# Four seven-product units per tile from tile 3, in a written-out order, with the second product begun on plain h and two subtractions on GpSimd

## The chip, the cores and the metric

One core of one Trainium2 chip. The time is the device time of one execution in microseconds, from runs of the same program; beside it there is one execution recorded by the hardware profiler. Engines are called PE (TensorE; PEld is its weight load), DVE (VectorE), ACT (ScalarE), POOL (GpSimd) and SP (SyncE, which here only issues output transfers).

## What is computed

Attention over pooled keys and values, and behind it a two-layer network with SiLU (8 batches, 8 heads, 576 positions, head size 64; pool 8, so 72 pooled rows; 4608 tokens, width 512, hidden width 2048):

```python
k_p = k.reshape(B, H, Sp, pool, D).mean(axis=3)
v_p = v.reshape(B, H, Sp, pool, D).mean(axis=3)
scores = np.matmul(q, k_p.transpose(0, 1, 3, 2)) / sqrt(D)
attn = softmax(scores)
x = matmul(attn, v_p)              # to [4608, 512], heads side by side
h = x @ w_in                       # [4608, 2048]
g = h * (1.0 / (1.0 + np.exp(-h)))
out = g @ w_out                    # [4608, 512], float32
```

All weights, x and g are held in bfloat16; sums are float32.

## The kernel before, in words

The tokens are cut in nine tiles of 512, `t` = 0 to 8. In each tile the *first product* (`up`) makes h_T = silu(x w_in), transposed, and the *second product* (`down`, `down_quarters`) makes the output rows. While tile t is worked on, the attention of batch a = t + 1 is fed in between, so that the columns of xT are there for tile t + 1. Tiles 7 and 8 have no attention in them, as there is no batch 8.

**Seven products for eight.** From tile 1 on, both products use a scheme in which a 2 x 2 block product takes seven block products in place of eight, at the price of sums of blocks before it and of results after it. The products are numbered 1 to 7. They accumulate in three PSUM tiles: P takes products 2, 4 and 7, Q takes 5, 3 and 6, R takes 1. Between them P and Q are copied out, so that one bank serves two purposes.

- In the *first product* such a scheme is a **unit**: four groups of 128 hidden columns by 512 tokens by the whole width of 512. `UNITS` names three of them: groups 4 to 7, 8 to 11 and 12 to 15. Each product of a unit is four matmuls of 256 columns (L477). ScalarE copies P after product 2 to r_sb (L494); VectorE forms rr_sb = Q + r_sb after product 5 (L497), t_sb = R - rr_sb after product 1 (L500), c_sb[0] = P + t_sb after product 7 (L509) and c_sb[1] = Q + t_sb after product 6 (L512); ScalarE makes four Silu (L485), two of PSUM after products 4 and 3, two of c_sb ("h" and "s" in the order's letters). The sums of weight blocks (`unit_weight_sum`, L437) are made once, in tiles 0 and 1; the sums of x blocks (`unit_x_sum`, L444) once per tile, five of them, at the end of the tile before.
- Groups 0 to 3 are made by `plain` (L537): four groups of four matmuls of 512 columns each, and one Silu each (L543).
- In the *second product* each of the seven products is 16 matmuls of 256 columns (L645). The left sides are sums of blocks of h_T (`hidden_sum`, L605: for products 2, 5, 1, 6 and 7), or h_T itself (products 4 and 3). The weight sums are in w_sum. The order is 2, 5, 1, 4, 3, 7, 6; r_sb, rr_sb and t_sb are used here too (L658, L660, L664), and the output rows are collected in o_sb (L666, L671, L675, L679) and stored by `store` (L549).

**Order.** The program is scheduled by hand: each engine runs its instructions in the order in which they are emitted. For tiles 2 to 8 the order of the first product's stages is a string (`THREE`: letter A, B, C for the unit and the numbers for the stages, "g0" for a plain group). All other work is a *filler*, emitted when a step counter (one step per matmul group) reaches its number: hidden sums, transposes of q (`q_transpose`, L159), scores and their exponentials (`scores`, L340, L348), denominators (`denominators`, L358, L367, L368), numerators with the multiplications that write xT (`numerators`, L384, L393), x sums, and the table loads of ScalarE (`attn_tables`, `moe_tables`).

**GpSimd.** From tile 2 on GpSimd pools k and v of batch a (`pool_k`, `pool_v`; L190, L193). It does so behind `behind_x_sums` (L196), a copy of one element that makes it wait for the last x sum. GpSimd also issues the loads: q of batch a + 1 (`load_q`, L151 and, for the last batch, eight small ones at L144), the first half of the raw k and v rows (`load_one`, L180), and the second half, added on by the transfer to the first, so it waits until that has landed (`load_rest`, L184).

**PSUM.** The 8 banks are two groups: "at" with five (scores, denominators, numerators, the units' P and Q) and "mm" with three (the units' R, plain groups, the second product's P, Q and R). A new tile takes the next bank of its group in turn and waits for the readers of what was there.

**SBUF buffers shared by both products:** r_sb, rr_sb, t_sb and c_sb exist once.

The visits of attention in a tile are three thirds of the positions; the third numerators of a batch are made one tile later than its others (`numerators(a - 1, visits[2])`).

Of the kernel before, what the change touches and what calls it, by code (L numbers as in the profile page):

```python
# [27 lines left out]
FP32 = mybir.dt.float32  # L28
# [8 lines left out]
def kernel(  # L37
# [9 lines left out]
    nc = tc.nc  # L47
# [43 lines left out]
    def ps_tile(shape, dtype, tag, name):  # L91
        return psum.tile(shape, dtype, tag=tag, bufs=banks[tag], name=name)
# [24 lines left out]
            singles.tile([128, 5, 2, 256], BF16, name=f"w_sum1{n}") for n in range(2)  # L117
        )
    ]
    x_sum = singles.tile([128, 5, 2, NQ], BF16, name="x_sum")  # L120
    gate = singles.tile([128, 1], BF16, name="gate")
    c_sb = [singles.tile([128, 2, NQ], FP32, name=f"c_sb{n}") for n in range(2)]
# [54 lines left out]
    def load_one(b, name):  # L177
        st = batches.setdefault(b, {})
        raw = raw_tile(f"{name}_raw", H)
        nc.gpsimd.dma_start(out=raw, in_=source(b, name)[:, :, :PH])  # L180
        st[f"{name}_raw"] = raw
# [10 lines left out]
        )  # L192
        nc.gpsimd.tensor_add(out=dst, in0=raw[:, :, :D], in1=raw[:, :, D : 2 * D])  # L193

    def behind_x_sums():
        nc.gpsimd.tensor_copy(out=gate[:1], in_=x_sum[:1, U_XI[6], 0, :1])  # L196

    def pool_k(b):
        pool_rows(kp[:SP], batches[b]["k_raw"])
# [119 lines left out]
    def third(n):  # L319
        return tuple((g, n * QV, (n + 1) * QV) for g in range(2))  # L320
# [78 lines left out]
    def attn_tables():  # L399
        nc.scalar.preload_act_table_set("natural_log_exp_and_others")  # L400
# [13 lines left out]

    UNITS = ((4, 6), (8, 10), (12, 14))
    UW = [
        {
            (i, j): w_in_sb[:, 2 * j : 2 * j + 2, 128 * u : 128 * (u + 2)]  # L420
# [14 lines left out]
    def unit_weight_sum(y, n):  # L435
        a, b = U_W[n]
        nc.vector.tensor_tensor(  # L437
            out=w_sum1[y][U_WI[n]], in0=UW[y][a], in1=UW[y][b],
            op=ALU.subtract if n in (6, 7) else ALU.add,
        )  # L440
# [19 lines left out]
    def up(t, fillers, items):  # L460
        step = spread(
            fillers,
            sum(
                KF if len(it) == 3 else 2 * len(it[1].strip("hs")) for it in items
            ),
        )
        ps = {}

        def product(y, n, bank, first):
            if first:  # L470
                tag = "mm" if bank == "R" else "at"
                ps[y, bank] = ps_tile([128, 2, NQ], FP32, tag, f"u_ps{bank}")
            w, x = unit_weights(y, n), unit_x(t, n)
            for u in range(2):
                next(step)
                for kk in range(2):
                    nc.tensor.matmul(  # L477
                        ps[y, bank][:, u, :], lhsT=w[:, kk, 128 * u : 128 * (u + 1)],
                        rhs=x[:, kk, :], start=first and u == 0 and kk == 0,
                        stop=kk == 1, skip_group_check=True,  # L480
                    )

        def hidden(y, i, j, src):
            g = UNITS[y][i]
            nc.scalar.activation(  # L485
                h_T[:, g : g + 2, j * NQ : (j + 1) * NQ], src, func=AF.Silu
            )

        tt = nc.vector.tensor_tensor

        def stage(y, n):
            if n == "2":
                product(y, 2, "P", True)
                nc.scalar.copy(r_sb, ps[y, "P"])  # L494
            elif n == "5":
                product(y, 5, "Q", True)
                tt(out=rr_sb, in0=ps[y, "Q"], in1=r_sb, op=ALU.add)  # L497
            elif n == "1":
                product(y, 1, "R", True)
                tt(out=t_sb, in0=ps[y, "R"], in1=rr_sb, op=ALU.subtract)  # L500
            elif n == "4":
                product(y, 4, "P", False)
                hidden(y, 1, 0, ps[y, "P"])
            elif n == "3":
                product(y, 3, "Q", False)
                hidden(y, 0, 1, ps[y, "Q"])
            elif n == "7":
                product(y, 7, "P", False)
                tt(out=c_sb[0], in0=ps[y, "P"], in1=t_sb, op=ALU.add)  # L509
            elif n == "6":  # L510
                product(y, 6, "Q", False)
                tt(out=c_sb[1], in0=ps[y, "Q"], in1=t_sb, op=ALU.add)  # L512
            elif n == "h":
                hidden(y, 0, 0, c_sb[0])
            else:
                hidden(y, 1, 1, c_sb[1])

        for it in items:
            if len(it) == 3:
                plain(t, step, *it)  # L520
            else:
                for n in it[1]:
                    stage(it[0], n)
        for _ in step:
            pass

    def plain(t, step, g, n0, n):
        tag = "at" if (t, g, n0) == (0, 3, 0) else "mm"
        hp_ps = ps_tile([128, 512], FP32, tag, "hp_ps")
        c0 = (t * NTT + n0) % NX  # L530

        for r0, r1 in ((0, min(n, NX - c0)), (min(n, NX - c0), n)):
            for kk in range(KF) if r1 > r0 else ():
                if r0 == 0:
                    next(step)
                x0 = (c0 + r0) % NX
                nc.tensor.matmul(  # L537
                    hp_ps[:, r0:r1],
                    lhsT=w_in_sb[:, kk, g * 128 : (g + 1) * 128],
                    rhs=xT[:, kk, x0 : x0 + r1 - r0],  # L540
                    start=(kk == 0), stop=(kk == KF - 1),
                )
        nc.scalar.activation(h_T[:, g, n0 : n0 + n], hp_ps[:, :n], func=AF.Silu)  # L543
# [58 lines left out]
    def hidden_sum(n, k0, k1):  # L602
        a, b, op = H_SUMS[n]
        ks = slice(k0, k1)
        nc.vector.tensor_tensor(  # L605
            out=h_sum[n][:, ks, :], in0=quarter(*a, ks), in1=quarter(*b, ks), op=op
        )
# [17 lines left out]
    def left(n, kt, c):  # L625
        cs = slice(128 * c, 128 * (c + 1))
        if n in h_sum:
            return h_sum[n][:, kt, cs]
        i = n - 3
        return h_T[:, i * KQ + kt, i * NQ + 128 * c : i * NQ + 128 * (c + 1)]  # L630
# [55 lines left out]
            pass  # L686


    warm_ps = ps_tile([128, 512], FP32, "mm", "warm_ps")

    def warm_up(n):
# [97 lines left out]
        " C6 Ch Cs g2 g3",  # L789
    )  # L790
    visits = [third(n) for n in range(3)]
    for t in range(NT):
        a = t + 1
        f_up, f_down = [], []
        if t == 0:
            GA = 11
            items = [(g, 0, HS) for g in range(GA)]
            items += [(g, HS, NTT - HS) for g in range(GA)]
            items += [(g, 0, NTT) for g in range(GA, KG)]
            f_up += [(1, lambda: denominators(0, part(0, 1), on_dve=True))]  # L800
            f_up += [(5, lambda: denominators(0, part(1, 1), on_dve=True))]
            f_up += [(13, lambda: numerators(0, part(0, 1)))]
            f_up += [(17, lambda: numerators(0, part(1, 1)))]
        else:
            G = lambda *gs: [(g, 0, NTT) for g in gs]
            if t == 1:
                items = (
                    G(12, 13, 14, 15) + [(0, "25143"), (1, "2"), (0, "7"), (1, "5")]
                    + [(0, "6h"), (1, "1")] + G(0) + [(1, "4"), (0, "s"), (1, "3")] + G(1)
                    + [(1, "7h6")] + G(2) + [(1, "s")] + G(3)  # L810
                )
            else:
                items = []
                for it in THREE[t // B].split():
                    items += [(("BCA".index(it[0])), it[1])] if it[0] in "ABC" else G(int(it[1]))
            if t == 1:
                for n in U_X:
                    f_up.append((0, lambda n=n: unit_x_sum(t, n)))
            for n in (2, 5):
                h_at = 50 if t == B else 54 if t > 1 else 45  # L820
                f_up.append((h_at, lambda n=n: hidden_sum(n, 4, 8)))
            f_up.append((56, lambda: hidden_sum(6, 4, 8)))
            for n, k0 in ((2, 0), (5, 0), (1, 4), (1, 0)):
                f_up.append((64, lambda n=n, k0=k0: hidden_sum(n, k0, k0 + 4)))
            f_down.append((33, lambda: hidden_sum(7, 0, 8)))
            f_down.append((71 if t < B else 50, lambda: hidden_sum(6, 0, 4)))

        for n, t0, f_to, at, parts in (
# [71 lines left out]
        if t == 1:  # L900
            def unit_weight_tiles():
                k_w = big.tile([128, 4, 2, 256], BF16, tag="k_raw2", name="w_sum12")
                v_w = big.tile([128, 4, 2, 256], BF16, tag="v_raw2", name="w_sum12")
                w_sum1.append([k_w[:, i] for i in range(4)] + [v_w[:, 0]])

            f_down.append((72, unit_weight_tiles))
            for i, n in enumerate(U_W):
                f_down.append((73 if i < 2 else 81, lambda n=n: unit_weight_sum(2, n)))
        if t != 1:
            moe_tables()  # L910
        if t == 0:
# [34 lines left out]
```

The softmax here doesn't subtract the row's maximum and nothing guards it: scores larger than these inputs give would overflow.

## Time and profile before

| | us |
|---|---|
| median of 7 runs | 279.87 (279.65 to 280.36) |
| the profiled execution: its own time | 279.9 |
| its span, first to last instruction | 278.1 |
| busy in the span: PE, PEld | 273.2, 203.2 |
| busy in the span: DVE, ACT, POOL | 220.6, 189.1, 98.4 |
| first-product matmuls of plain groups, L537 | 268 |
| window 139.34 to 168.12, a tile with attention: PE, DVE, ACT, POOL | 28.78, 23.30, 22.11, 11.92 |

A busy time is the union of an engine's instructions. On DVE and ACT an instruction of 0.69 us is followed by the next after 0.60, since they overlap a little; on PE the printed end of a matmul is modelled and lies beyond the start of the next. "x4" counts instructions of a merged row. A row of a wait is: engine, what it waited to run, what ended the wait, us in total, times, longest.

### The profile page before, as it was taken

The page shows a single profiled execution, that of the slowest core. Times are in us where ns is not written, and L with a number is a line of the kernel's source. Part 1 is how long each engine was busy: PE and PEld are TensorE (multiplying, and loading weights), DVE is VectorE, ACT ScalarE, POOL GpSimd, SP SyncE. Part 2 cuts the span into 40 slices and gives each one's busy share as a digit, 9 for nine tenths or more (in the row PEclk, how much of TensorE's full clock was granted, in tenths as well). Part 3 has the DMA queues.
Part 4 walks back from the last instruction along what each step waited for, and adds up shares of the span by engine and source line. Part 5 has one row for each costly group of instructions (what it writes and reads, how often), then busy time and mean ns, then how long its engine had stood idle before and what let it go on. Part 6 is the DMA issues. An engine that isn't in the chain of part 4 may idle for free.

```text
span 278.1 us, 7160 instructions
## 1 busy us (share of the span) xinstructions
PE 273.2 (98%) x2877; PEld 203.2 (73%) x2877; DVE 220.6 (79%) x415; ACT 189.1 (68%) x369; POOL 98.4 (35%) x104
## 2 busy tenths in 40 slices
PE   8999999999999999999999999999999999999995
PEld 4458444576778677867888788687877778788784
DVE  4985787788998976897689768986888588966982
ACT  1688767468577966797679757985799478326810
POOL 8745217242158430953086207970640000000001
PEclk9999999999999999999999999999999999999999
DMA  7999999896759888579746835599610041005004
GB/s 208 289 260 241 206 325 181 228 177 122 148 69 221 211 116 163 129 178 130 145 109 180 127 67 133 132 136 132 148 47 2 2 104 50 0 11 136 7 2 152
DMA packets 31313, 37.71 MB, mean 136 GB/s; under 512 B 10352, under 2 KB 22256, under 8 KB 31280
## 3 DMA queue, kind: packets, MB, share of 16 engines
q0 software_dynamic: 23920, 27.03, 52.8%
q1 hardware_dynamic: 6928, 9.58, 12.5%
q10 hardware_dynamic: 432, 0.66, 0.7%
q8 instruction: 22, 0.36, 0.5%
q14 instruction: 11, 0.09, 0.1%
HBM read 36.70 MB, written 9.44 MB: 166 GB/s over the span
## 4 chain that ended last, share of the span: by engine, by line
PE 79%; DMA 12%; DVE 3%; POOL 2%; issue 1%; ACT 1%; POOLq 0%
PE o_psQ L645 15%; PE o_psP L645 15%; PE u_psP L477 11%; PE u_psQ L477 11%; PE hp_ps L537 10%; DMA w_in_sb<-in_moe_w_in_dram 6%; DMA w_out_sb<-in_moe_w_out_dram 6%; PE o_psR L645 5%; PE u_psR L477 4%; PE sc_ps L340 3%; PE nu_ps L384 3%; PE o_ps L572 2%; PE den_ps L358 2%; DVE h_sum L605 1%; POOL q_bf L133 1%
## 5 line engine op out<-in xcount | busy, mean ns | idle before, releaser
L645 PEld LDWEIGHTS <-h_sum 128*128 128x128 bf16 x640 | 60.7, 98 | 11.5 <-DVE h_sum L605 1.3
L477 PEld LDWEIGHTS <-w_sum 128*128 128x128 bf16 x460 | 45.0, 98 | 8.2 <-issue 0.2
L605 DVE TENSOR_TENSOR h_sum<-h_T 128x1024 bf16<-128x1024 bf16 (+1 forms) x72 | 49.7, 742 | 1.6 <-ACT h_T L543 1.0
L537 PE MATMUL hp_ps<-xT,w_in_sb 128*128 128x512 bf16 (+3 forms) x268 | 50.3, 332 | 0.0
L348 ACT ACTIVATE es<-sc_ps 72x384 bf16<-72x384 f32 (+1 forms) x100 | 39.0, 469 | 8.5 <-PE sc_ps L340 8.3
L543 ACT ACTIVATE h_T<-hp_ps 128x512 bf16<-128x512 f32 (+2 forms) x63 | 31.6, 520 | 10.0 <-PE hp_ps L537 8.5
L537 PEld LDWEIGHTS <-w_in_sb 128*128 128x128 bf16 x268 | 25.6, 98 | 15.1 <-issue 0.7
L485 ACT ACTIVATE h_T<-c_sb 128x512 bf16<-128x512 f32 x46 | 28.8, 628 | 4.4 <-DVE c_sb L509 3.6
L393 DVE TENSOR_TENSOR xT<-nu_ps,rec 128x384 bf16<-128x384 f32 (+1 forms) x50 | 24.0, 532 | 4.9 <-PE nu_ps L384 4.8
L645 PEld LDWEIGHTS <-h_T 128*128 128x128 bf16 x256 | 24.1, 98 | 4.5 <-issue 0.9
L549 POOL DMA_DIRECT2D out_dram<-o_sb x2 | 1.2, 617 | 67.9 <-issue 67.2
L367 ACT ACTIVATE lnd<-den_ps 128x384 f32<-128x384 f32 (+1 forms) x23 | 11.1, 483 | 19.6 <-PE den_ps L358 19.6
L190 POOL TENSOR_TENSOR raw<-raw 72x1024 f32<-72x1024 f32 x10 | 23.6, 2364 | 0.1
L500 DVE TENSOR_TENSOR t_sb<-u_psR,rr_sb 128x512 f32<-128x512 f32 x23 | 15.9, 692 | 6.7 <-PE u_psR L477 5.0
L494 ACT COPY r_sb<-u_psP 128x512 f32<-128x512 f32 x23 | 13.4, 585 | 10.7 <-PE u_psP L477 8.0
L477 PEld LDWEIGHTS <-w_in_sb 128*128 128x128 bf16 x184 | 17.6, 98 | 2.4
L497 DVE TENSOR_TENSOR rr_sb<-u_psQ,r_sb 128x512 f32<-128x512 f32 x23 | 15.7, 681 | 4.0 <-ACT r_sb L494 2.1
L645 PE MATMUL o_psP<-w_out_sb,h_sum 128*128 128x256 bf16 x128 | 17.6, 273 | 0.0
L512 DVE TENSOR_TENSOR c_sb<-u_psQ,t_sb 128x512 f32<-128x512 f32 x23 | 15.8, 686 | 2.3 <-PE u_psQ L477 2.1
L509 DVE TENSOR_TENSOR c_sb<-u_psP,t_sb 128x512 f32<-128x512 f32 x23 | 15.8, 685 | 1.8 <-PE u_psP L477 0.9
L645 PE MATMUL o_psQ<-w_sum,h_sum 128*128 128x256 bf16 x128 | 16.7, 273 | 0.0
L645 PE MATMUL o_psQ<-w_out_sb,h_sum 128*128 128x256 bf16 x128 | 16.6, 273 | 0.0
(83 smaller groups left out, 510.6 us busy)
## 6 DMA issues: line engine op xcount, KB each, us to landing
out_dram<-o_sb SPq DMA_DIRECT2D x128, 64.0 KB, 1.9
raw<-in_k_dram POOLq DMA_DIRECT2D x10, 576.0 KB, 8.0
raw<-in_v_dram POOLq DMA_DIRECT2D x10, 576.0 KB, 8.1
q_bf<-in_q_dram POOLq DMA_DIRECT2D x6, 576.0 KB, 10.9
w_in_sb<-in_moe_w_in_dram POOLq DMA_DIRECT2D x8, 256.0 KB, 8.6
w_out_sb<-in_moe_w_out_dram POOLq DMA_DIRECT2D x4, 512.0 KB, 13.3
raw<-in_v_dram POOLq DMA_DIRECT2D x2, 768.0 KB, 10.9
raw<-in_k_dram POOLq DMA_DIRECT2D x1, 768.0 KB, 10.8
```

Source lines behind the costliest of these rows:

```text
L190: nc.gpsimd.tensor_add(out=raw[:, :, : 2 * D], in0=raw[:, :, : 2 * D], in1=raw[:, :, 2 * D :])
L348: nc.scalar.activation(es[:, s, :], sc[s], func=AF.Exp, scale=score_scale)
L393: nc.vector.tensor_mul(out=xT[:, 2 * g0 + c : 2 * (g0 + ng - 1) + c + 1 : 2, cols], in0=nu[c][:, :w].rearrange("r (g n) -> r g n", g=ng), ...
L477: nc.tensor.matmul(ps[y, bank][:, u, :], lhsT=w[:, kk, 128 * u : 128 * (u + 1)], rhs=x[:, kk, :], start=first and u == 0 and kk == 0, stop ...
L485: nc.scalar.activation(h_T[:, g : g + 2, j * NQ : (j + 1) * NQ], src, func=AF.Silu)
L500: tt(out=t_sb, in0=ps[y, "R"], in1=rr_sb, op=ALU.subtract)
L509: tt(out=c_sb[0], in0=ps[y, "P"], in1=t_sb, op=ALU.add)
L512: tt(out=c_sb[1], in0=ps[y, "Q"], in1=t_sb, op=ALU.add)
L537: nc.tensor.matmul(hp_ps[:, r0:r1], lhsT=w_in_sb[:, kk, g * 128 : (g + 1) * 128], rhs=xT[:, kk, x0 : x0 + r1 - r0], start=(kk == 0), stop= ...
L543: nc.scalar.activation(h_T[:, g, n0 : n0 + n], hp_ps[:, :n], func=AF.Silu)
L605: nc.vector.tensor_tensor(out=h_sum[n][:, ks, :], in0=quarter(*a, ks), in1=quarter(*b, ks), op=op)
L645: nc.tensor.matmul(ps[b][:, c, :], lhsT=left(n, kt, c), rhs=W_OUT[n][:, kt, :], start=b not in begun, stop=kt == k1 - 1, skip_group_check= ...
```

## The change

From tile 3 on, each tile is emitted by a new function, `run`, from one string of tokens (`PROGRAM`), instead of by `up`, `down_quarters` and fillers:

- A fourth unit, groups 0 to 3 (`UNITS` gets (0, 2)), takes the place of the four plain groups. Its weight sums are made in tile 2, into buffers `w_e` and the rest of `v_w`. In the tokens, A, B, C, E are the units (4, 6), (8, 10), (12, 14), (0, 2), with the stage behind the letter ("a" is the Silu of c_sb[0], "s" that of c_sb[1]).
- The second product is done by `down_stages` in quarters ("d40" is the first quarter of product 4), in the order 4, 3, 2, 5, 1, 7, 6. Products 4 and 3, whose left side is h_T itself, come first. r_sb and rr_sb then hold product 4 and the sum of 4 and 3, before P and Q go on with products 2 and 5; so that t_sb's sum gets the same value, what P and Q have become is taken off rr_sb by two subtractions ("u1", "u2") that GpSimd runs.
- Hidden sums are tokens ("h2h" and "h2l": upper and lower half of product 2's); that of product 7 is in two halves. x sums are "x7 x1 x4 x3 x6": two ahead of product 6, three inside and behind it. The third numerators of the batch before ("npp") and three of the four q transposes are in the first product. In tile 6, "nu2" is added at the end.
- In the last tile, products 4, 3, 2, 5 are whole, and 1, 7, 6 follow by halves of the output rows (`columns`).
- All GpSimd work of a tile but the subtractions is emitted at its beginning.
- In tile 1 the hidden sum of product 7 goes from step 33 to 44 of the second product.

```diff
+    w_e = singles.tile([128, 2, 2, 256], BF16, name="w_sum1e")
...
-    UNITS = ((4, 6), (8, 10), (12, 14))
+    UNITS = ((4, 6), (8, 10), (12, 14), (0, 2))
...
+    def down_stages(t, last):
+        ps = {}
+        bank = {2: "P", 5: "Q", 1: "R", 4: "P", 3: "Q", 7: "P", 6: "Q"}
+        begun = set()
+        add, sub = ALU.add, ALU.subtract
+        tt = nc.vector.tensor_tensor
+
+        def matmuls(n, k0, k1, cs=(0, 1)):
+            b = bank[n]
+            for kt in range(k0, k1):
+                for c in cs:
+                    nc.tensor.matmul(
+                        ps[b][:, c, :], lhsT=left(n, kt, c), rhs=W_OUT[n][:, kt, :],
+                        start=b not in begun,
+                        stop=kt == k1 - 1, skip_group_check=True,
+                    )
+                    begun.add(b)
+
+        def after(n, cc=(0, 1), tail=False):
+            cs = slice(cc[0], cc[-1] + 1)
+            if n == 4:
+                nc.scalar.copy(r_sb, ps["P"])
+            elif n == 3:
+                tt(out=rr_sb, in0=ps["Q"], in1=r_sb, op=add)
+            elif n == 2:
+                nc.scalar.copy(o_sb[1][:, :, LO], ps["P"])
+                if last:
+                    store(t, 3, LO, (nc.gpsimd,))
+            elif n == 5:
+                nc.vector.tensor_copy(out=o_sb[0][:, :, HI], in_=ps["Q"])
+                if last:
+                    store(t, 1, HI)
+            elif n == 1:
+                tt(out=t_sb[:, cs], in0=ps["R"][:, cs], in1=rr_sb[:, cs], op=add)
+            elif n == 7:
+                tt(out=o_sb[0][:, cs, LO], in0=ps["P"][:, cs], in1=t_sb[:, cs], op=add)
+                for c in cc:
+                    store(t, c, LO if tail else FULL, (nc.scalar if tail else nc.sync,))
+            else:
+                tt(out=o_sb[1][:, cs, HI], in0=ps["Q"][:, cs], in1=t_sb[:, cs], op=add)
+                for c in cc:
+                    if tail:
+                        store(t, 3, HI, both)
+                    else:
+                        store(t, 2 + c, FULL, (nc.gpsimd if last else nc.sync,))
+
+        def part_of(tok):
+            if tok == "o":
+                return after(6)
+            n = int(tok[1])
+            if tok[0] == "u":
+                src = o_sb[1][:, :, LO] if n == 1 else o_sb[0][:, :, HI]
+                nc.gpsimd.tensor_tensor(out=rr_sb, in0=rr_sb, in1=src, op=sub)
+                return
+            if not ps:
+                for b in "PQR":
+                    ps[b] = ps_tile([128, 2, CQ], FP32, "mm", f"o_ps{b}")
+            i = int(tok[2])
+            k0 = 2 * i if n == 4 else 2 * (i ^ 2)
+            matmuls(n, k0, k0 + 2)
+            if i == 3 and n != 6:
+                after(n)
+
+        def columns(c):
+            for n in (1, 7, 6):
+                matmuls(n, 0, KQ, (c,))
+                after(n, (c,), c == 1)
+
+        return part_of, columns
+
+    PROGRAM = (
+        "C2 C5 q3 C1 B2 C4 B5 q2 C3 q0 A2 B4 C7 Ca B3 C6 B1 A4 A5 Cs B7 E2 B6 A1 Ba A3 "
+        "E5 A7 Bs E4 A6 E3 Aa E1 npp As E7 k Ea E6 Es h2h d40 d41 q1 h5h h7l d42 d43 "
+        "d30 d31 d32 T1 h2l d33 sc0 h5l h1h h1l h7h d20 d21 d22 d23 sc1 de0 d50 d51 d52 "
+        "d53 d10 u1 sc2 h6h de1 h6l d11 u2 d12 d13 d70 nu0 nu1 de2 d71 d72 T2 d73 x7 x1 "
+        "d60 d61 x4 d62 d63 x3 x6 o "
+    )
+
+    def run(t):
+        a = t + 1
+        attn, last = a < B, t == NT - 1
+        stage = unit_stages(t, iter(int, 1))
+        part_of, columns = down_stages(t, last)
+        toks = PROGRAM.split()
+        gate_on = int([x for x in toks if x[0] == "x"][-1][1])
+        attn_toks = ("T1 T2 k npp q0 q1 q2 q3 sc0 sc1 sc2 de0 de1 de2 nu0 nu1").split()
+        if last:
+            i = toks.index("d10")
+            sums = [x for x in toks[i:] if x[0] in "hu"]
+            toks = toks[:i] + sums + ["L0", "L1"]
+        toks = [x for x in toks if attn or x not in attn_toks]
+        if a == B - 1:
+            toks.insert(1 + max(toks.index("de2"), toks.index("nu1"), toks.index("o")), "nu2")
+        if t == T4:
+            toks.insert(0, "T2")
+        if attn:
+            if a + 1 < B - 1:
+                load_q(a + 1)
+            behind_x_sums(6 if t == T4 else gate_on)
+            pool_k(a)
+            if a + 1 < B:
+                load_one(a + 1, "k")
+            pool_v(a)
+            if a + 1 < B:
+                load_one(a + 1, "v")
+                if a + 1 == B - 1:
+                    load_q(a + 1)
+                load_rest(a + 1, "k")
+                load_rest(a + 1, "v")
+        for x in toks:
+            if x[0] in "ABCE" and x[1] in "2514376as":
+                stage("ABCE".index(x[0]), {"a": "h"}.get(x[1], x[1]))
+            elif x[0] == "L":
+                columns(int(x[1]))
+            elif x[:2] == "de":
+                denominators(a, visits[int(x[2])])
+            elif x[0] in "dou":
+                part_of(x)
+            elif x[0] == "h":
+                k0 = 4 if x[2] == "h" else 0
+                hidden_sum(int(x[1]), k0, k0 + 4)
+            elif x == "T1":
+                attn_tables()
+            elif x == "T2":
+                moe_tables()
+            elif x == "k":
+                k_transpose(a)
+            elif x == "npp":
+                numerators(a - 1, visits[2])
+            elif x[0] == "q":
+                n = int(x[1])
+                q_transpose(a, n % 2, n // 2)
+            elif x[:2] == "sc":
+                scores(a, visits[int(x[2])])
+            elif x[:2] == "nu":
+                numerators(a, visits[int(x[2])])
+            elif not last:
+                unit_x_sum(t + 1, int(x[1]))
 
     warm_ps = ps_tile([128, 512], FP32, "mm", "warm_ps")
 
...
         " C6 Ch Cs g2 g3",
     )
     visits = [third(n) for n in range(3)]
+    T4 = 3
     for t in range(NT):
         a = t + 1
+        if t >= T4:
+            run(t)
+            continue
         f_up, f_down = [], []
         if t == 0:
             GA = 11
...
             f_up.append((56, lambda: hidden_sum(6, 4, 8)))
             for n, k0 in ((2, 0), (5, 0), (1, 4), (1, 0)):
                 f_up.append((64, lambda n=n, k0=k0: hidden_sum(n, k0, k0 + 4)))
-            f_down.append((33, lambda: hidden_sum(7, 0, 8)))
+            f_down.append((33 if t > 1 else 44, lambda: hidden_sum(7, 0, 8)))
             f_down.append((71 if t < B else 50, lambda: hidden_sum(6, 0, 4)))
 
         for n, t0, f_to, at, parts in (
...
                 k_w = big.tile([128, 4, 2, 256], BF16, tag="k_raw2", name="w_sum12")
                 v_w = big.tile([128, 4, 2, 256], BF16, tag="v_raw2", name="w_sum12")
                 w_sum1.append([k_w[:, i] for i in range(4)] + [v_w[:, 0]])
+                w_sum1.append([v_w[:, 1 + i] for i in range(3)] + [w_e[:, i] for i in range(2)])
 
             f_down.append((72, unit_weight_tiles))
             for i, n in enumerate(U_W):
                 f_down.append((73 if i < 2 else 81, lambda n=n: unit_weight_sum(2, n)))
+        if t == 2:
+            for i, n in enumerate(U_W):
+                f_down.append((76 + 2 * i, lambda n=n: unit_weight_sum(3, n)))
         if t != 1:
             moe_tables()
         if t == 0:
```

The stages of a unit and the loop over them, which were inside `up`, are split off as `unit_stages`, unchanged.

## Prediction

> **What bounds the kernel now.** I read the page's part 1 first, then TensorE's own waits, then the busy time by tile, then the order of time at two places. On the page, TensorE is busy for 98% of the span at full granted clock:
>
> ```profile
> PE 273.2 (98%) x2877; PEld 203.2 (73%) x2877; DVE 220.6 (79%) x415; ACT 189.1 (68%) x369; POOL 98.4 (35%) x104
> PEclk9999999999999999999999999999999999999999
> ```
>
> A busy PE is not PE at its peak, so I ask for its waits. The view has three lines, all of them from before tile 1:
>
> ```profile
> PE warm_ps L693 <- DVE warm L712: 1.2, 1, 1.2
> PE kz_ps L285 <- DVE k L267: 0.2, 1, 0.2
> PE o_ps L572 <- DMA w_out_sb<-in_moe_w_out_dram: 0.2, 1, 0.2
> ```
>
> By tile (window; busy of PE, PEld, DVE, ACT, POOL), a tile with attention lasts 28.73 us, all of it TensorE, with 23.3 us of VectorE and 22.1 us of ScalarE beside it:
>
> ```profile
> 110.61:139.34 28.73, 28.73 (x327) 22.69 (x325) 23.30 (x42) 22.09 (x43) 12.68 (x10) 1.00 0.74 143
> 168.12:196.85 28.73, 28.73 (x325) 22.62 (x324) 23.30 (x43) 22.09 (x43) 17.30 (x17) 1.00 0.98 138
> ```
>
> TensorE in order of time at a seam between two tiles gives its two prices. The second column overlaps the next entry, so I take start to start:
>
> ```profile
> 167.08 0.60 PE L477 MATMUL u_psP<-xT,w_sum 128*128 128x256 bf16 x4
> 167.52 0.60 PE L477 MATMUL u_psQ<-xT,w_sum 128*128 128x256 bf16 x4
> 167.96 1.03 PE L537 MATMUL hp_ps<-xT,w_in_sb 128*128 128x512 bf16 x4
> 168.82 0.60 PE L477 MATMUL u_psP<-xT,w_sum 128*128 128x256 bf16 x4
> ```
>
> One product of a unit (four matmuls of 256 columns) takes 0.437 us and one plain group (four of 512) 0.86 us. So in tiles 2 to 8 time is TensorE work and nothing else, as long as its suppliers keep up.
>
> [...]
>
> **The change, part by part.**
>
> *Fourth unit (tiles 3 to 8).* Removed: four plain groups, 4 x 0.865 = 3.46 us of TensorE. Added: seven products, 7 x 0.437 = 3.06 us. That is 0.40 us a tile; in tile 4, whose columns wrap (139.18 to 140.05 for one group), 0.44. Six tiles: 5 x 0.40 + 0.44 = **2.45 us saved**. Since nothing else bounds these tiles it reaches the end unless a supplier falls behind. The same attention matmuls remain in as many groups.
>
> *What the fourth unit asks of the others.* VectorE gets four 128x512 operations (L497, L500, L509, L512: 0.69 each, 0.60 start to start): 4 x 0.60 = 2.4 us, so 25.7 of a 28.3 us tile, 91%. ScalarE swaps four Silu for four and adds a copy of 0.585 and slower reads of c_sb (0.63 for 0.60): 22.8 of 28.3. Neither is a bound by its sum; what counts is whether each result is there in time, so I walk one tile by hand, with 0.25 us from a product's end to the reader's start (product at 142.67 to 143.11, reader at 143.38). Call the end of the last product 7 zero.
>
> *Seam.* TensorE: product 6 to 1.75, then C2, C5, C1, B2, C4, B5, C3 of the next tile at 0.437 each, so C3 starts at 4.37 and overwrites Q, which needs C's rr_sb sum. VectorE: o_sb LO sum 0.2 to 0.8, five x sums (1.75 us in the row below) to 2.55, o_sb HI sum to 3.15, rr_sb sum ends 3.85. Slack 0.5 us. Before, the same chain stood in this order:
>
> ```profile
> 166.44 1.76 DVE L444 TENSOR_TENSOR x_sum<-xT 128x512 bf16<-128x512 bf16 x5
> 168.12 0.68 DVE L679 TENSOR_TENSOR o_sb<-o_psQ,t_sb 128x512 f32<-128x512 f32 x1
> 168.72 0.68 DVE L497 TENSOR_TENSOR rr_sb<-u_psQ,r_sb 128x512 f32<-128x512 f32 x1
> ```
>
> *First product.* The 28 products, the moved third numerators (16 matmuls, 0.43; two multiplications of 0.49 on VectorE) and the k transposes (0.12) end at 14.5. The tightest places are E3 (rr_sb sum 0.4 us early) and B3 (0.6 early). Three of the four q transposes (0.4 each, no DMA issue) stand among the first ten products and fit there.
>
> *Second product.* Starting with plain h, products 4 and 3 fill 3.5 us before any hidden sum is needed. VectorE comes out of the first product 1.6 us late (numerators, then c_sb twice); h2h, q1, h5h, h7l, h2l follow and h2l ends at 4.5 after TensorE's end; its reader d22 starts at 4.83. Slack 0.3 us, the smallest of the walk. The later sums are 1 us or more early. The ten hidden sums cost what the nine of before did (halving product 7's, 1.21, gives two of 0.60). The score exponentials stay 0.5 us or more ahead of their banks' next use; table loads and their number stay.
>
> *Two subtractions on GpSimd.* [...] They lie beside products 5 to 1. [...] I take no stall.
>
> *GpSimd's queue.* It runs loads first: the last issues of a tile are these.
>
> ```profile
> 139.63 2.35 POOL L190 TENSOR_TENSOR raw<-raw 72x1024 f32<-72x1024 f32 x1
> 154.93 1.39 POOL L184 DMA_DIRECT2D raw<-in_v_dram  x1 [2.68 <-DMA raw<-in_v_dram]
> 186.40 1.97 POOL L184 DMA_DIRECT2D raw<-in_v_dram  x1
> ```
>
> That is 19.5 us after the seam's zero in tiles 3 and 4 and 22.6 in tile 5 (eight q loads); the first subtraction is wanted at 21.0 and may start at 22.6. The next tile's q load (one issue, 1.31 us) moves from ahead of the tile's end to behind the second subtraction, some 6 us later; it lands in 10.9 us and is read a tile later. SP's 16 output issues a tile keep their order.
>
> *Fourth unit's weight sums (tile 2).* Five of 0.34 start to start: two before the wait of 1.05 at L671, three before the 1.11 at L675. Hidden; without that cover 1.7 us would go through to the seam.
>
> *Product 7's hidden sum in tile 1, step 33 to 44.* Tile 1 has a small gap: the numerators wait for the cast of v, which stands behind this 1.21 us sum.
>
> ```profile
> 72.52 0.35 PE L358 MATMUL den_ps<-es,ones 72*32 72x384 bf16 x4
> 72.84 0.76 PE L384 MATMUL nu_ps<-es,vp 72*32 72x192 bf16 x16
> 73.54 0.94 PE L645 MATMUL o_psP<-w_sum,h_T 128*128 128x256 bf16 x7
> 71.24 1.21 DVE L605 TENSOR_TENSOR h_sum<-h_T 128x2048 bf16<-128x2048 bf16 x1
> 72.37 0.74 DVE L310 CAST vp<-v_ps 72x256 bf16<-72x256 f32 x2
> ```
>
> From 72.52 to 73.54 is 1.02 us; the same two groups elsewhere (164.93 to 165.54) take 0.61. With the cast first, **0.4 us saved**; the sum then fills VectorE until the t_sb sum, as before.
>
> *Last tile.* New: its order is products 4, 3, 2, 5 whole (7.0 us after the first product), then 1, 7, 6 by columns, so product 6 starts at 8.73. Its hidden sums stand behind the o_sb HI copy (7.2 to 7.8): they end at 9.1, **0.4 us late**. [...] I take 1.0 lost. The tail behind the last product (3.1 us) has the same three short operations and stores.
>
> **Sum**, against the profiled execution: 279.9 (span 278.1 and 1.8 around it; the median of the runs is 279.87, so no correction). 279.9 - 2.45 - 0.4 + 1.0 = 278.05, say **278.0**.
>
> **Rivals.** [...] *Slower: GpSimd's queue.* The subtractions sit behind load_rest, which waits for DMA; that wait was up to 7.1 us in one tile. t_sb's sum then holds VectorE's queue: attention multiplications, x sums, and so the next tile's C1. It decides from about 1.6 us of lateness in tile 5 and 3.5 in tiles 3 and 4; 1.2 us of stall in three tiles gives 281.6. Against it: the waits in these tiles were 1.2 to 3.1 us and q's load is the only transfer that moves. That the unit doesn't save TensorE time I exclude: its products have the form of those already measured.
>
> **Chances.** Forecast 0.42, free 0.27, lock at the seams 0.16, queue or another missed arrival 0.15. With 0.2% as 0.56 us, which is about what a measurement of this kernel tells from no change: the first two are faster, half of the third is no change and most of the rest of it faster: faster 0.76, same 0.09, slower 0.15. The range goes from the free case with no loss to just short of the slower one: 276.8 to 280.0.
>
> **What would show it.** Right: tiles 3 to 6 at 28.3 us and TensorE without waits there; hidden sums of the last tile ahead of a TensorE gap of 0.4 to 1.6 us; subtractions near 1.2 us. Wrong: a gap ahead of C3 or d22 in every tile, x sums late, or GpSimd's subtractions starting over 22.6 us after the seam.

## The result and the profile after

The changed kernel takes 280.84 us (median of 15 runs) where the kernel before takes 280.11 us beside it: a ratio of 1.0028 (95% interval 1.0021 to 1.0034). It is **slower by 0.8 us** by the ratio, 0.7 by the two medians. The forecast was 278.0 us, with 280.0 as the upper end. The profiled execution took 280.92 us, with a span of 279.1.

Page, part 1, and the waits of TensorE (who waited for whom: us in total, times, longest), changed kernel:

```profile
PE 272.3 (98%) x2933; PEld 209.1 (75%) x2933; DVE 243.5 (87%) x449; ACT 190.7 (68%) x373; POOL 117.3 (42%) x116
```

```profile
PE o_psQ L705 <- DVE h_sum L610: 1.7, 1, 1.7
PE warm_ps L837 <- DVE warm L856: 1.2, 1, 1.2
PE o_ps L577 <- DMA w_out_sb<-in_moe_w_out_dram: 0.4, 1, 0.4
```

One new wait has come in, 1.7 us, once. It is the last tile's. That explains the loss but not why the saving of 2.45 us is missing. For that I go tile by tile, from the start of a tile's first product to that of the next (tile 8: to the end of its last product), all from the order of time on TensorE:

| tile | before | changed | difference |
|---|---|---|---|
| 2 | 28.74 | 28.74 | 0.00 |
| 3, 4, 5 | 28.73, 28.77, 28.73 | 28.65, 28.66, 28.66 | -0.08, -0.11, -0.07 |
| 6 | 29.29 | 29.20 | -0.09 |
| 7 | 24.87 | 24.67 | -0.20 |
| 8 | 24.86 | 26.56 | +1.70 |

With the 0.41 us that tile 1 gains, the sum is +0.74 us; the interval above is 0.6 to 1.0 us. The two profiled spans differ by 1.0: in the changed kernel's execution tile 0's wait for w_out lasted 0.35 us at L577, where it was 0.16 at L572 before; tile 0 lies ahead of everything that the change touches.

Windows of the changed kernel (busy of PE, PEld, DVE, ACT, POOL), to be read against those of before: TensorE still fills the tile but for 0.05 us, VectorE has gone from 23.3 to 26.5 us.

```profile
138.03:166.69 28.66, 28.61 (x338) 23.78 (x336) 26.47 (x47) 22.61 (x43) 15.30 (x11) 1.00 0.61 124
166.69:195.35 28.66, 28.61 (x339) 23.79 (x337) 26.47 (x47) 22.61 (x43) 20.18 (x19) 1.00 0.99 139
```

"Still fills" deceives: the printed end of a matmul is modelled (0.60 us for a product that the next follows after 0.44) and covers short gaps. They show only from start to start. TensorE in tile 4, at unit E's products 6, 3 and 1:

```profile
148.08 0.60 PE L489 MATMUL u_psQ<-x_sum,w_sum 128*128 128x256 bf16 x4
148.72 0.60 PE L489 MATMUL u_psQ<-x_sum,w_in_sb 128*128 128x256 bf16 x4
149.16 0.60 PE L489 MATMUL u_psR<-x_sum,w_sum 128*128 128x256 bf16 x4
```

From the first (the last product of unit A) to the second (E's product 3) it is 0.64 us, where every other step is 0.44. This **0.21 us** is there in each of tiles 3 to 8. E's product 3 overwrites what E's rr_sb sum reads, and VectorE at that time runs t_sb of A, rr_sb of E, and c_sb twice:

```profile
147.16 0.69 DVE L512 TENSOR_TENSOR t_sb<-u_psR,rr_sb 128x512 f32<-128x512 f32 x1
147.98 0.69 DVE L509 TENSOR_TENSOR rr_sb<-u_psQ,r_sb 128x512 f32<-128x512 f32 x1
148.59 0.68 DVE L521 TENSOR_TENSOR c_sb<-u_psP,t_sb 128x512 f32<-128x512 f32 x1
149.18 0.68 DVE L524 TENSOR_TENSOR c_sb<-u_psQ,t_sb 128x512 f32<-128x512 f32 x1
```

The rr_sb sum ends at 148.67 and product 3 starts at 148.72. Start to start the four operations are 0.82, 0.61 and 0.59: the rr_sb sum, which overwrites what the t_sb sum ahead of it has just read, starts 0.2 us later than an independent one would. Ahead of these four, VectorE waited for TensorE for the last time at c_sb[1] of unit C:

```profile
143.54 0.69 DVE L524 TENSOR_TENSOR c_sb<-u_psQ,t_sb 128x512 f32<-128x512 f32 x1 [0.18 <-PE u_psQ L489]
```

From there to E's rr_sb sum at 147.98 it takes six steps in 4.44 us. Two of them are 0.60; the other four, each of an operation that overwrites what the one ahead of it reads (t_sb or rr_sb), are 0.79 to 0.83.

The last tile in order of time, all engines:

```profile
268.71 2.97 POOL L746 TENSOR_TENSOR rr_sb<-rr_sb,o_sb 128x512 f32<-128x512 f32 x2
268.85 0.69 DVE L723 COPY o_sb<-o_psQ 128x512 f32<-128x512 f32 x1 [0.16 <-PE o_psQ L705]
269.45 2.77 DVE L610 TENSOR_TENSOR h_sum<-h_T 128x1024 bf16<-128x1024 bf16 x2
269.52 1.04 PE L705 MATMUL o_psP<-w_sum,h_sum 128*128 128x256 bf16 x8
272.28 1.05 PE L705 MATMUL o_psQ<-w_sum,h_sum 128*128 128x256 bf16 x8 [1.73 <-DVE h_sum L610]
```

Product 7's first column starts at 269.52 and takes 0.87; product 6 follows at 272.28, so 1.89 us are lost. Its two hidden sums last 2.77 us, beside both subtractions on GpSimd. Two causes are possible: the sums' position behind the copy of product 5's result, and what the expectations below call the lock, a GpSimd instruction and VectorE's sums holding each other up. The lock was an assumption of mine ahead of the experiments; no run had shown it.

### The profile page after: what moved, and what is told of

Read it like the earlier page. It is cut to its first block, busy times and chain, and to the rows that moved or that the text cites. A ratio compares the mean times of both kernels' runs of the same rounds, so it can differ in the third digit from the quotient of the medians.

```text
span 279.1 us, 7369 instructions
## 1 busy us (share of the span) xinstructions
PE 272.3 (98%) x2933; PEld 209.1 (75%) x2933; DVE 243.5 (87%) x449; ACT 190.7 (68%) x373; POOL 117.3 (42%) x116
## 4 chain that ended last, share of the span: by engine, by line
PE 73%; DMA 12%; DVE 8%; issue 3%; POOL 2%; DVEq 0%; POOLq 0%
PE o_psQ L705 11%; PE o_psP L705 11%; PE u_psP L489 10%; PE u_psQ L489 9%; DMA w_in_sb<-in_moe_w_in_dram 6%; DMA w_out_sb<-in_moe_w_out_dram 6%; PE o_psQ L650 4%; PE o_psP L650 4%; PE hp_ps L542 4%; PE u_psR L489 4%; PE o_psR L705 4%; DVE t_sb L512 3%; PE sc_ps L341 3%; PE nu_ps L385 3%; PE o_ps L577 2%
## 5 line engine op out<-in xcount | busy, mean ns | idle before, releaser
L610 DVE TENSOR_TENSOR h_sum<-h_T 128x1024 bf16<-128x1024 bf16 (+1 forms) x78 | 58.4, 798 | 1.6 <-ACT h_T L548 1.0
L489 PEld LDWEIGHTS <-w_sum 128*128 128x128 bf16 x532 | 52.0, 98 | 7.2 <-issue 0.3
L705 PEld LDWEIGHTS <-h_sum 128*128 128x128 bf16 x480 | 45.6, 98 | 10.0 <-issue 2.3
L497 ACT ACTIVATE h_T<-c_sb 128x512 bf16<-128x512 f32 x58 | 35.6, 627 | 8.7 <-DVE c_sb L521 8.4
L746 POOL TENSOR_TENSOR rr_sb<-rr_sb,o_sb 128x512 f32<-128x512 f32 x12 | 20.0, 1665 | 42.7 <-ACT o_sb L719 38.8
L542 PE MATMUL hp_ps<-xT,w_in_sb 128*128 128x512 bf16 (+2 forms) x156 | 26.6, 319 | 0.0
L548 ACT ACTIVATE h_T<-hp_ps 128x512 bf16<-128x512 f32 (+2 forms) x39 | 18.1, 476 | 5.8 <-PE hp_ps L542 5.1
L497 ACT ACTIVATE h_T<-u_psQ 128x512 bf16<-128x512 f32 x29 | 17.1, 590 | 3.3 <-PE u_psQ L489 3.1
L497 ACT ACTIVATE h_T<-u_psP 128x512 bf16<-128x512 f32 x29 | 17.4, 599 | 2.2 <-PE u_psP L489 2.1
L489 PE MATMUL u_psQ<-x_sum,w_in_sb 128*128 128x256 bf16 x116 | 17.5, 272 | 0.3
```

The source lines that it names most:

```text
L489: nc.tensor.matmul(ps[y, bank][:, u, :], lhsT=w[:, kk, 128 * u : 128 * (u + 1)], rhs=x[:, kk, :], start=first and u == 0 and kk == 0, stop ...
L497: nc.scalar.activation(h_T[:, g : g + 2, j * NQ : (j + 1) * NQ], src, func=AF.Silu)
L542: nc.tensor.matmul(hp_ps[:, r0:r1], lhsT=w_in_sb[:, kk, g * 128 : (g + 1) * 128], rhs=xT[:, kk, x0 : x0 + r1 - r0], start=(kk == 0), stop= ...
L610: nc.vector.tensor_tensor(out=h_sum[n][:, ks, :], in0=quarter(*a, ks), in1=quarter(*b, ks), op=op)
L705: nc.tensor.matmul(ps[b][:, c, :], lhsT=left(n, kt, c), rhs=W_OUT[n][:, kt, :], start=b not in begun, stop=kt == k1 - 1, skip_group_check= ...
L746: nc.gpsimd.tensor_tensor(out=rr_sb, in0=rr_sb, in1=src, op=sub)
```

## The experiments

Each ran on one chip together with the kernel before, and its ratio is to that; the changed kernel's 1.0028 is the mark that they are read against (one thousandth is 0.28 us).

**1. Last tile: subtractions on VectorE.**

```diff
-                nc.gpsimd.tensor_tensor(out=rr_sb, in0=rr_sb, in1=src, op=sub)
+                eng = nc.vector if last else nc.gpsimd
+                eng.tensor_tensor(out=rr_sb, in0=rr_sb, in1=src, op=sub)
...
-            toks = toks[:i] + sums + ["L0", "L1"]
+            toks = toks[:i] + sorted(sums) + ["L0", "L1"]
```

> The changed kernel, with one edit in the last tile alone: the two subtractions run on VectorE, behind both hidden sums of product 6, instead of on GpSimd. Theory A (lock): no GpSimd operation reads SBUF beside the sums, so these take 0.60 and 0.68 us and not 1.4 each; what is left of the gap of 1.9 us is the backlog of the copy, about 0.4 us; time 1.5 us below the changed kernel, 279.3 beside 280.1 of before. Theory C (position only: the sums are late because they stand behind the copy, and GpSimd costs nothing): the gap stays 1.9 us and the time 280.8.

280.32 us, ratio 1.0011 (1.0003 to 1.0019). VectorE and TensorE in the last tile:

```profile
268.97 0.69 DVE L723 COPY o_sb<-o_psQ 128x512 f32<-128x512 f32 x1 [0.16 <-PE o_psQ L705]
269.58 1.28 DVE L610 TENSOR_TENSOR h_sum<-h_T 128x1024 bf16<-128x1024 bf16 x2
```

```profile
269.65 1.04 PE L705 MATMUL o_psP<-w_sum,h_sum 128*128 128x256 bf16 x8
270.92 1.05 PE L705 MATMUL o_psQ<-w_sum,h_sum 128*128 128x256 bf16 x8 [0.24 <-DVE h_sum L610]
272.78 1.03 PE L705 MATMUL o_psR<-w_sum,h_sum 128*128 128x256 bf16 x8 [0.81 <-DVE t_sb L727]
```

The sums fall from 2.77 to 1.28 us, so GpSimd cost them 1.5 us, and the gap is 0.40 us (270.92 - 269.65 - 0.87). So the lock makes 1.5 us of the gap and the position 0.4. But the time fell by 0.5 us and not 1.5: a second wait has come up, 0.99 us (272.78 - 270.92 - 0.87). Product 1's second column waits for the t_sb sum, which reads the first column of the same PSUM tile and now stands behind both subtractions.

**2. The same, and ScalarE copies product 5's result.**

```diff
-                nc.vector.tensor_copy(out=o_sb[0][:, :, HI], in_=ps["Q"])
+                copy = nc.scalar.copy if last else nc.vector.tensor_copy
+                copy(out=o_sb[0][:, :, HI], in_=ps["Q"])
```

> The changed kernel, with two edits in the last tile alone: the two subtractions run on VectorE behind both hidden sums of product 6, and ScalarE (idle there) copies product 5's result, which VectorE copied ahead of those sums. Theory A (VectorE's backlog plus the lock with GpSimd hold the sums up): both are gone, the sums end about 1.3 us after the end of product 5, ahead of the 1.75 us at which TensorE wants them; the gap of 1.9 us ahead of product 6 goes whole, and the time falls by 1.9 us, to 278.9 beside 280.1 of the kernel before. Theory B (the gap comes from something else, such as TensorE waiting for the bank or for weights): it stays, 280.8.

279.66 us, ratio 0.9985 (0.9977 to 0.9993). The gap ahead of product 6 is gone, as theory A has it; 0.60 us is left at the second column of product 1, so the gain is 1.2 us and not 1.9.

**3. All subtractions on VectorE.**

```diff
-                nc.gpsimd.tensor_tensor(out=rr_sb, in0=rr_sb, in1=src, op=sub)
+                nc.vector.tensor_tensor(out=rr_sb, in0=rr_sb, in1=src, op=sub)
```

> The changed kernel with both subtractions on VectorE in all of its tiles, at the same places of the order. Theory A: the hidden sums of product 6 fall from 2.35 to 1.3 us in tiles 3 to 7, the two subtractions add about 1.3 us, so those tiles stay at 28.65 us; in the last tile the gap falls from 1.9 to about 1.0 us, since one subtraction now stands ahead of the sums: 280.0, 0.8 us below the changed kernel. Theory C (GpSimd takes real load off VectorE and the lock costs little): 1.3 us more VectorE work per tile pushes the sums at the seam past product 3 of unit C, some 0.5 us in four tiles, 282 or more.

280.56 us, ratio 1.0013 (1.0007 to 1.0020). Tiles 3 to 5 stay at 28.66 us, and the last gap is 1.00 us, as reckoned. The total falls by 0.4 us by the ratios (0.3 by the medians) and not 0.8: tile 7 takes 0.10 us more, at product 3 of unit C, where theory C looked for it, and in the last tile 0.26 us comes up at the second column of product 1. Product 6's two sums in tile 4 take 2.35 us in the changed kernel:

```profile
157.88 1.80 POOL L746 TENSOR_TENSOR rr_sb<-rr_sb,o_sb 128x512 f32<-128x512 f32 x1 [1.75 <-ACT o_sb L719]
160.37 2.35 DVE L610 TENSOR_TENSOR h_sum<-h_T 128x1024 bf16<-128x1024 bf16 x2
160.59 1.58 POOL L746 TENSOR_TENSOR rr_sb<-rr_sb,o_sb 128x512 f32<-128x512 f32 x1 [0.92 <-DVE o_sb L723]
```

and 1.29 in this run, between the two subtractions:

```profile
160.13 0.68 DVE L746 TENSOR_TENSOR rr_sb<-rr_sb,o_sb 128x512 f32<-128x512 f32 x1
160.73 1.29 DVE L610 TENSOR_TENSOR h_sum<-h_T 128x1024 bf16<-128x1024 bf16 x2
161.94 0.68 DVE L746 TENSOR_TENSOR rr_sb<-rr_sb,o_sb 128x512 f32<-128x512 f32 x1
```

So the second subtraction, which GpSimd runs beside hidden sums, costs VectorE about 1.06 us; one that VectorE runs itself costs it a step of 0.60 us, or of 0.79 where the t_sb sum behind it reads its result. Moving the second one to GpSimd takes nothing off VectorE. The first falls in part into a wait that VectorE has anyhow, in tile 4 1.21 us ahead of the copy of product 5's result in the changed kernel and 1.20 in this run.

**4. Second buffers for rr_sb and t_sb, in the output buffers.**

```diff
+            second = t >= 3 and y % 2
+            rr, ts = (o_sb[0][:, :, HI], o_sb[1][:, :, LO]) if second else (rr_sb, t_sb)
```

> The changed kernel from tile 3 on, with the units B and E of the first product forming their sums rr_sb and t_sb in other buffers (halves of the output buffers, which are free then), so that the sum of one unit does not overwrite what the sum just before it on VectorE has read. Theory A (each overwriting costs VectorE about 0.2 us, since the next sum starts 0.8 us after its predecessor and not 0.6; over a tile the chain falls behind until the rr_sb sum of unit E comes 0.2 us after TensorE wants its bank): the gap of 0.21 us ahead of E's product 3 goes in all six tiles, 1.3 us less, 279.6 beside 280.1 of before. Theory B (the rr_sb sum of E waits for ScalarE's copy or for a result of TensorE): the gap stays and the time is 280.8.

308.91 us, ratio 1.1046 (1.1014 to 1.1078): a miss, and my mistake. I took these halves to be free once the last tile was stored, but VectorE waited for its output transfers (up to 4.8 us at one sum). The run says nothing on the theory.

**5. The same, in memory that no transfer touches.** The two buffers lie in product 7's hidden sum.

```diff
+        spare = h_sum[7].rearrange("p k n -> p (k n)").bitcast(FP32).rearrange(
+            "p (i c n) -> p i c n", i=2, c=2
+        )
...
+            rr, ts = (spare[:, 0], spare[:, 1]) if t >= T4 and y % 2 else (rr_sb, t_sb)
```

> The changed kernel from tile 3 on, with units B and E of the first product forming rr_sb and t_sb in the memory of product 7's hidden sum, which nothing reads at that time and no transfer touches. Theory A (a sum that overwrites what VectorE's sum just before it has read starts 0.8 us after it and not 0.6; this lateness adds up until unit E's rr_sb sum comes 0.2 us too late for its product 3): VectorE's steps inside the units fall to 0.6 us, the gap ahead of E's product 3 goes in six tiles, 1.3 us less than the changed kernel: 279.6 beside 280.1 of before. Theory B (E's rr_sb sum waits for ScalarE's copy or TensorE): gap and time stay, 280.8.

279.66 us, ratio 0.9981 (0.9974 to 0.9989), 1.3 us below the changed kernel by the ratios and 1.2 by the medians, as theory A has it. VectorE at the same four operations as above (E's rr_sb sum is printed under the name of the memory that it is in now, h_sum):

```profile
146.75 0.68 DVE L517 TENSOR_TENSOR t_sb<-u_psR,rr_sb 128x512 f32<-128x512 f32 x1
147.45 0.69 DVE L514 TENSOR_TENSOR h_sum<-u_psQ,r_sb 128x512 f32<-128x512 f32 x1
148.06 0.68 DVE L526 TENSOR_TENSOR c_sb<-u_psP,t_sb 128x512 f32<-128x512 f32 x1
148.76 0.69 DVE L529 TENSOR_TENSOR c_sb<-u_psQ,t_sb 128x512 f32<-128x512 f32 x1
```

The step from t_sb to the next rr_sb sum is 0.70 in place of 0.82, the one from c_sb to t_sb 0.61 in place of 0.79 (146.14 to 146.75; 146.37 to 147.16 in the changed kernel). The 0.70 is a wait: E's product 5 starts at 146.75, and its reader starts 0.70 us later, as the reader of unit A's product 5 does (144.13 and 144.83). VectorE has caught up with TensorE. The gap ahead of E's product 3 is gone in all tiles; they take 28.45 us (3 to 5), and tile 7 takes 24.47: 0.40 us below before, which is the unit's saving exactly.

**6. Another order: E's product 1 ahead of its product 3.**

```diff
-E4 A6 E3 Aa E1 npp
+E4 A6 E1 Aa E3 npp
```

> The changed kernel with one edit of the written-out order: unit E's product 1 ahead of its product 3, so that TensorE does 0.44 us of other work before it needs E's rr_sb sum. Theory A (that sum is 0.2 us late and nothing else): the gap goes in all six tiles; products 3 and 7 keep their place for what follows, 1.3 us less: 279.6 beside 280.1. Theory D (VectorE as a whole is behind in the first product and any reorder only moves the gap): a gap of 0.2 us turns up at another place, such as the fourth quarter of product 4 or the first of product 2, and the time is 280.8.

280.98 us, ratio 1.0037 (1.0024 to 1.0049): no gain. Tiles 3 to 5 fall to 28.45 us, as A has it. But tiles 7 and 8 have a new gap, as D has it, though longer and behind another engine. TensorE in tile 7, E's products 7 and 6:

```profile
235.16 0.60 PE L489 MATMUL u_psP<-x_sum,w_sum1e 128*128 128x256 bf16 x4
236.25 0.60 PE L489 MATMUL u_psQ<-x_sum,w_sum1e 128*128 128x256 bf16 x4 [0.49 <-ACT h_T L497]
```

The step is 1.09 us, 0.65 too much: product 6 adds to the bank whose product 3 ScalarE is still reading, from 235.62 for 0.58 us. With attention, numerators and k transposes stand between the two products, and no such gap shows. Tiles 3 to 6 gain 0.21 us each, tiles 7 and 8 lose 0.44 each.

**7. Only what comes ahead of tile 3.**

```diff
-    T4 = 3
+    T4 = NT
```

> The kernel before with what the change does ahead of tile 3 only: product 7's hidden sum of tile 1 moved from step 33 to 44, and the fourth unit's weight sums made in tile 2 (and not used). Theory A: the wait of tile 1's numerators for the cast of v goes (0.41 us) and the weight sums are hidden in VectorE's waits: 279.7 beside 280.1 of before. Theory B: later work takes the 0.41 us back, or the weight sums cost up to 1.7 us: 280.1 to 281.4.

279.77 us, ratio 0.9989 (0.9981 to 0.9997). In tile 1 the denominators and numerators take 0.61 us (72.64 to 73.25) where it was 1.02, and tile 2 takes 28.74 us with its five weight sums: theory A.

**8. Plain groups in the new order.**

```diff
...
+            g = {"E2": "g0", "E5": "g1", "E4": "g2", "E3": "g3"}.get(x)
+            if g or x[0] != "E":
+                toks.append(g or x)
...
+            elif x[0] == "g":
+                plain(t, iter(int, 1), int(x[1]), 0, NTT)
```

> The changed kernel with the four plain groups 0 to 3 of the kernel before in the place of the fourth unit (at the places of its products 2, 5, 4 and 3); all else of the new order stays. Reckoning: a tile with attention takes 28.73 (before) plus what the new order of attention costs, which I put at 0.12 us (the difference between the 28.45 us of the tile without the gap and 28.73 - 0.40): 28.85 us; tile 7 takes 24.87 us; the gap of 1.9 us in the last tile stays, since it hangs on the copy behind product 5 and not on the first product. 280.1 - 0.4 + 4 x 0.12 + 1.9 = 282.1, 1.2 us over the changed kernel, which is what the unit brings there net of its own gap (6 x 0.19). Rival: the unit brings nothing net, since VectorE is the bound: 280.8 or less.

282.20 us, ratio 1.0078 (1.0064 to 1.0092); tiles 3 to 5 take 28.85, 28.88 and 28.85 us and the last gap is 1.98: as reckoned. The unit brings 1.4 us net of its own gap (reckoned: 1.2), and the new order of attention costs 0.12 us a tile.

**9. All mends together.** The edits of experiments 1, 2 and 5, and a PSUM tile of its own for the second half of product 1 in the last tile:

```diff
+            if c == 1:
+                ps["R"] = ps_tile([128, 2, CQ], FP32, "at", "o_psR2")
+                begun.discard("R")
```

> The changed kernel with the second buffers of units B and E, and in the last tile both subtractions on VectorE behind the hidden sums, the copy of product 5's result on ScalarE, and product 1's second half of rows in a PSUM bank of its own, so that it doesn't wait for the reader of the first half. If the two gaps (six of 0.21 us and one of 1.9) are all that the change lost beside its attention order: 280.8 - 1.3 - 1.9 = 277.7 beside 280.1 of before, a ratio of 0.991. If the gaps only hide others behind them, it stays above 279.

**277.66 us, ratio 0.9915 (0.9901 to 0.9928)**, as reckoned: the best version, 2.4 us below the kernel before. Tile 8 takes 24.52 us, 0.34 below before. With both gaps gone, the unit's 2.45 us, tile 1's 0.41 and the attention order's 0.48 the other way make 2.4.

**10. Denominators beside numerators**, on top of 9:

```diff
-d10 u1 sc2 h6h de1 h6l d11 u2 d12 d13 d70 nu0 nu1 de2 d71
+d10 u1 sc2 h6h h6l d11 u2 d12 d13 d70 de1 nu0 de2 nu1 d71
```

> The version with all mends, with the second and third denominators directly ahead of numerators (de1 nu0 de2 nu1). Theory A: the new order's 0.12 us a tile is the three denominators, which take 0.27 us of TensorE where a full-size matmul follows and 0.17 where numerators follow (in the kernel before two of three stood so); moving two of them saves 0.1 us each, some 0.2 us in tiles 3 to 6: 276.9, ratio 0.989. Rival: ScalarE's later logarithms hold up the numerators' banks or the multiplications, and 0.3 us or more a tile is lost: 278.9 or more.

277.93 us, ratio 0.9925 (0.9912 to 0.9937): no gain, and the tiles stay at 28.45 us. TensorE in tile 4 of this run:

```profile
162.07 0.35 PE L359 MATMUL den_ps<-es,ones 72*32 72x384 bf16 x4
162.24 0.50 PE L385 MATMUL nu_ps<-es,vp 72*32 72x192 bf16 x16
162.57 0.34 PE L359 MATMUL den_ps<-es,ones 72*32 72x384 bf16 x4
162.73 0.62 PE L385 MATMUL nu_ps<-es,vp 72*32 72x192 bf16 x16
163.29 1.49 PE L710 MATMUL o_psP<-w_sum,h_sum 128*128 128x256 bf16 x12
```

The two denominators did fall to 0.17 us each, but what stands around them counts too. The fair measure is from the start of a stretch of attention matmuls to the next full-size matmul. In tile 4:

| stretch | before | all mends (9) | this order (10) |
|---|---|---|---|
| scores | 0.47, 0.47 | 0.47 | 0.47, 0.47 |
| scores and a denominator | 0.75 | 0.74, 0.75 | 0.75 |
| 16 numerators | | 0.45 | 0.45 |
| 16 numerators and a denominator | 0.61 | | |
| 32 numerators and a denominator | 0.94 | 0.94 | |
| 32 numerators and two denominators, as above | | | 1.22 |
| sum | 3.24 | 3.35 | 3.36 |

A denominator adds 0.28 us to scores, 0.16 at the edge of numerators and 0.28 between two groups of them (1.22 - 0.94). Before, two of three stood at the edge of numerators; in the new order it is one. That is 0.11 of the 0.12 us a tile, so theory A had the price right, and this experiment gained nothing because it put one denominator at an edge and the other in between. This is read from the traces; an order that keeps two at the edges was not run, and why the neighbours matter stays open.

## Why the prediction was wrong

- **The fourth unit** saves 0.40 us of TensorE a tile, as worked out (tile 7 of experiment 5). The step that failed is the supplier's: "0.69 each, 0.60 start to start", and with it "the tightest places are E3 (rr_sb sum 0.4 us early)". Two of the four operations of a unit overwrite what the operation ahead of them reads and start 0.8 us after it, so a unit costs VectorE 2.8 us and not 2.4. By its sum that still fits the 3.06 that TensorE gives it; what fails is the walk. The six steps up to E's rr_sb sum take 4.44 us and not 3.6, and it is 0.2 us late instead of 0.4 early: 6 x 0.21 = 1.3 us. Experiment 5 shows it by taking the overwriting away. What holds an overwriting operation back for 0.2 us is not shown. I took the step from pairs that were independent, and the 0.60 given with the profile before is that of such pairs alone. The trace before held the other one, 0.82 in tile 4:

```profile
145.05 0.69 DVE L500 TENSOR_TENSOR t_sb<-u_psR,rr_sb 128x512 f32<-128x512 f32 x1
145.87 0.69 DVE L497 TENSOR_TENSOR rr_sb<-u_psQ,r_sb 128x512 f32<-128x512 f32 x1
```

- **"The same attention matmuls remain in as many groups"**: true of their number, but they cost 0.12 us a tile more, 0.5 us in all. It was costed at nothing without adding up the groups' steps: one more denominator stands beside scores (experiment 10).
- **The last tile**: the prediction has its hidden sums 0.4 us late by their position and takes 1.0 us lost. No run shows that 1.0; the runs showed 1.89, of which experiment 1 gives the position's part as 0.40 and the lock's as 1.5. The 1.0 is the middle of the 0.4 to 1.6 that the prediction names as the gap to look for; splitting the difference between two ends was no estimate. Both subtractions ran beside the sums: GpSimd's issue of an output transfer, 0.66 us from 268.03 on, stands ahead of the first, and my walk had left it out.
- **The subtractions**: no run before the change shows a price near 1.2 us for this shape, which GpSimd did not run there. It was right for the shortest (1.26, in tile 3, where the four hidden sums beside it took 3.58 us for the 2.48 of tile 4), but most take 1.6 to 2.3 beside hidden sums, which fits the lock seen from its other side. The second one cost VectorE 1.06 us. No stall at the seam: right. GpSimd's queue: right; in tile 5 the first starts at 186.53, just behind the loads, and nothing waits for it.
- **Tile 1** (0.41 us) and **tile 2's weight sums** (hidden): right.
- The sum with the measured terms: - 2.45 + 1.27 + 0.48 - 0.41 + 1.89 = +0.8 us, which is what the runs show. Of the 2.6 us between this and the forecast change of -1.85, E's rr_sb sum makes 1.3, the last tile 0.9 and the attention order 0.5. Of the rivals, neither "lock at the seams" nor "GpSimd's queue" (281.6) came about: the seams and the queue held, and the first product did not.

What the runs show of the lock is this: the hidden sums, with two SBUF inputs, go from 1.28 us a pair (experiment 1) to 2.77 beside GpSimd's subtractions, and the copy from PSUM ahead of them takes 0.69 us in both. What makes them hold each other up is not shown.

## What to carry to other kernels

When an engine's work is squeezed in under another's, walk its queue with the step from start to start of *each pair* as it stands, and take apart pairs where the second overwrites what the first reads: here two spare buffers brought 1.2 us. A sum of busy time that fits is not enough. TensorE's short gaps (0.21 us in each of six tiles here) were not in its list of waits; add up its steps per stage. Before moving work to GpSimd, look at what VectorE runs beside it: here a subtraction moved beside sums with two SBUF inputs cost VectorE 1.06 us where it had cost 0.60 to 0.79. And look above all at the last tile, where nothing comes behind to hide a late sum (1.89 us here).

## What was not expected of the hardware

TensorE ran slow for a while behind a long wait. In experiment 4, after 3.91 us of waiting:

```profile
122.78 0.60 PE L489 MATMUL u_psQ<-x_sum,w_in_sb 128*128 128x256 bf16 x4 [3.91 <-DVE rr_sb L511]
123.38 1.01 PE L489 MATMUL u_psQ<-xT,w_sum 128*128 128x256 bf16 x4
124.19 1.06 PE L489 MATMUL u_psP<-x_sum,w_sum 128*128 128x256 bf16 x4
```

The steps go from 0.44 to 0.6, then 0.81 to 0.86 four times over, then back: some 1.8 us lost. The clock row of the page, in 40 slices of 7.66 us, has this stretch and a second one:

```profile
PEclk9999999999999999799999999599999999999999
```

The 7 is the slice from 122.6 to 130.2 us, the 5 the one from 191.5 to 199.2; all others are at 9. TensorE's list of waits has twelve for the two buffers' sums, six of up to 3.9 us and six of up to 3.2, so most of them have no such stretch behind them. These waits (12.6 and 8.7 us, 21.3 together) and the 1.8 us make most of the 28 us over the changed kernel; the rest I did not take apart. What lowered the clock is not shown. The mean granted clock of that execution was 0.983, and 0.972 to 0.983 in all six of this kernel; in the runs of the other kernels it was 0.997 or more.
